# A chunk's transposed outputs in the bytes of its own sums

## The chip, the cores and the metric

The kernel runs on one core of a Trainium2 chip. The metric is the time of one execution in device microseconds, the median of several runs. Besides, one execution was taken by the hardware profiler; its trace is what the rows below are from.

## What is computed

Two independent blocks share the launch, and their outputs stand side by side. Block A is sliding-window attention over 2048 tokens, 32 heads of 32 columns, a window of 256 keys; block B is a Fourier mixing by matrix products.

```python
q, k, v = split(x @ wqkv)                       # x: 2048 x 1024
scores = (q @ k.T) * Dh ** -0.5                 # mask: 0 <= query - key < 256
a = (softmax(scores) @ v) @ wo
y = re(DFT_seq) @ (xb @ DFT_hid_re.T) - im(DFT_seq) @ (xb @ DFT_hid_im.T)
out = concatenate([a, y], axis=-1)
```

## The kernel before

The big products (q, k and v, then block B, then `wo`) are float16 products of split operands: each float32 operand is a high and a low half, and three passes of 128x512 matmuls make one product. The attention is a generator, `attention()`, which `tick` advances between these matmuls, a step every few matmuls by a rate per unit. So the attention's instructions are woven into the stream of each engine in an order that the code fixes; TensorE works through its list in that order.

The attention goes over *blocks* (g, hp, sc, i): eight groups g of four heads, two head pairs hp, four chunks sc of 512 queries, four blocks i of 128 queries. Four blocks that share (g, hp, sc) make a *chunk*; there are 64 chunks and 256 blocks. For each block b:

- `s_step`: TensorE makes the scores of both heads (`s`, and `far` for the oldest key block; two halves of one bank alternate as `far`), VectorE masks them with `far` (`copy_predicated`, L259) and takes the row maximum, ScalarE takes exponentials and the high half, VectorE the low half (`hl`, L275), and a DMA issued from SP transposes both into `t` (L277).
- `z_step`: GpSimd masks two triangles (`z`, L289, and `t`, L291).
- `v_step`, six blocks later (`LAG`) and for two blocks at once: TensorE multiplies with v into `pv`, and VectorE reduces the halves into the chunk's sums `o` (L323). A chunk has two such reduces; the first one allocates `o`.
- `o_step`, right after a chunk's second reduce: VectorE takes the reciprocals of the row sums (L332), GpSimd multiplies (L334), ScalarE takes the high half (L337) and GpSimd the low half (L338) into `ohl`, a DMA issued from SP transposes `ohl` into `ot` (L340).
- The store of `ot` to DRAM (`ots`, L360) is issued from SP about three blocks later, at the next block with i = 3. The last chunks' stores follow at once.

`o`, `ohl` and `ot` are tiles of the pool `att` under one tag, `"o"`, with three buffers of 1056 bytes per partition. Which of the three a tile gets is decided while the program is built. In the program before, `ohl` is always in the same buffer, and `o` and `ot` share the other two: for most chunks all `o` lie in one and all `ot` in the other, and at some chunks they change places, `ot` lying where the chunk's own `o` lay. A tile that takes a buffer over waits until the last instructions that used the buffer are done: the store for `ot`, and GpSimd's subtraction (L338) for `o`.

SP issues all loads, transpositions and most stores, in the order of the code; a wait in it holds up what stands behind. After the attention and block B, the pool `late` takes the memory of `att`, and the product with `wo` ends the kernel.

Of the kernel before, what the change touches and what calls it, by code (L numbers as in the profile page):

```python
# [9 lines left out]
F32 = mybir.dt.float32  # L10
F32R = mybir.dt.float32r
F16 = mybir.dt.float16
# [7 lines left out]
P = 128  # L20
# [3 lines left out]
DH = 32  # L24
# [6 lines left out]
QB = CH // P  # L31
# [22 lines left out]
def fused_kernel(ctx: ExitStack, tc: tile.TileContext, xa, wqk, wv, wo, xb, wd, cs, out):  # L54
    nc = tc.nc
# [57 lines left out]
    def mm(*args, **kwargs):  # L113
        with tc.issue_after(fixed[0].ins) if fixed else nullcontext():
            fixed[:] = [nc.tensor.matmul(*args, **kwargs)]  # L115
        return fixed[0]
# [94 lines left out]
    def attention():  # L211
        att = cell["att"]
# [3 lines left out]
        st, cur, q2s, k2s, vts, store_o = {}, {}, {}, {}, {}, []  # L216
# [78 lines left out]
        def v_step(b):  # L295

            g, hp, sc, i = blocks[b]
            pvb = ps_v.tile([P, CH], F32, tag="pv", name=f"pv_{b}")
            pvt = pvb[:, :4 * VW].rearrange("p (r h w) -> p r h w", r=2, h=2)
            if (g, hp, sc) not in cur:  # L300
                cur[g, hp, sc] = att.tile([P, QB, 2, DH + 1], F32, tag="o", bufs=3, name=f"o_{g}_{hp}_{sc}")
            for r in (1, 0):
                qb = sc * QB + i + r
                nb = min(qb + 1, 3)
                nt = min(nb, 2)
                d = st[b + r]

                def weights(part, j, kb):
                    if nb == 3 and kb == 0:
                        return d["z"][:, part * 2 + j]  # L310
                    return d["t"][:, (part * 2 + j) * nt + kb - (nb - nt)]

                seq = [(0, kb) for kb in range(nb)] + [(1, kb) for kb in range(nb)]
                for j in range(2):
                    at = j * VW
                    for m, (part, kb) in enumerate(seq):
                        w = VW if part == 0 else DH + 1
                        k = qb + 1 - nb + kb
                        mm(pvt[:, r, j, :w], weights(part, j, kb),
                           vts[g, hp, k // QB][:, k % QB, at:at + w],  # L320
                                         start=(m == 0), stop=(m == len(seq) - 1),
                                         skip_group_check=True)
            nc.vector.tensor_reduce(cur[g, hp, sc][:, i:i + 2], pvt.rearrange("p r h (k w) -> p r h w k", k=2),  # L323
                                    axis=AX.X, op=ALU.add)
            del st[b], st[b + 1]

        def o_step(g, hp, sc):

            o = cur.pop((g, hp, sc))
            rs = att.tile([P, 2 * QB], F32, tag="rs", name=f"rs_{g}_{hp}_{sc}")  # L330
            on = o.rearrange("p i h w -> p (i h) w")
            nc.vector.reciprocal(rs, on[:, :, DH])  # L332
            on = on[:, :, :DH]
            nc.gpsimd.tensor_tensor(on, on, rs.unsqueeze(2).to_broadcast([P, 2 * QB, DH]), op=ALU.mult)  # L334
            o = o[:, :, :, :DH]
            ohl = att.tile([P, QB, 2, DH, 2], F16, tag="o", bufs=3, name=f"ohl_{g}_{hp}_{sc}")
            nc.scalar.activation(ohl[:, :, :, :, 0], o, AF.Copy)  # L337
            nc.gpsimd.tensor_tensor(ohl[:, :, :, :, 1], o, ohl[:, :, :, :, 0], op=ALU.subtract)  # L338
            ot = att.tile([P, QB, P], F16, tag="o", bufs=3, name=f"ot_{g}_{hp}_{sc}")
            nc.sync.dma_start_transpose(ot, ohl.rearrange("p i h d a -> p (i h d a)"))  # L340
            store_o.append((ots[sc, g, hp].rearrange("c a t -> (c a) t"), ot.rearrange("p i q -> p (i q)")))

        for b in range(nblk + LAG):
            for j in range(2):
                yield (blocks[b][0], blocks[b][2]) if b < nblk else None
                if b < nblk and j == 0:
                    s_step(b, 0)
                    s_step(b, 1)
                if j == 1 and b % 2 == 0 and b >= LAG:
                    v_step(b - LAG)  # L350
                    g, hp, sc, i = blocks[b - LAG + 1]
                    if i == QB - 1:
                        o_step(g, hp, sc)
                if j == 1 and b % 2 == ZAT and 3 <= b < nblk + 4:
                    for m in (b - 3 - (ZAT == 0), b - 2 - (ZAT == 0)):
                        if 0 <= m < nblk:
                            z_step(m)
                if j == 1 and store_o and (b >= nblk or blocks[b][3] == 3):
                    with tc.issue_after(line[0].ins):
                        nc.sync.dma_start(*store_o.pop(0))  # L360
                if j == 1 and b < nblk and blocks[b][3] == 1 and b + 3 < nblk:
                    g, hp, sc, _ = blocks[b + 3]
                    if (g, sc) in ready:
                        do_load(g, hp, sc)
                if j == 1 and b < nblk and blocks[b][3] == 3 and b + 1 < nblk:
                    g, hp, sc, _ = blocks[b + 1]
                    if (g, sc) in ready:
                        do_load_v(g, hp, sc)
# [526 lines left out]
    with tc.tile_pool(name="pa", bufs=3) as pa:  # L895
# [43 lines left out]
        for n, (kd, g, c) in enumerate(order):  # L939
# [12 lines left out]
            if kd == "v":  # L952
# [6 lines left out]
                f = vf[:, g, t // 4:t // 4 + 1]  # L959
# [137 lines left out]
    with tc.tile_pool(name="pb", bufs=1) as pb:  # L1097
# [45 lines left out]
        for n, (kind, p, c, i) in enumerate(units):  # L1143
# [35 lines left out]
            f = fu.pop(n)  # L1179
# [75 lines left out]
```

## Time and profile before

| | us |
|---|---|
| median of 3 runs | 1704.11 |
| lowest and highest of them | 1701.39, 1705.67 |
| the profiled execution | 1701.5 |
| its span in the trace | 1699.8 |
| TensorE busy in the span | 1688.6 |
| VectorE busy | 1299.0 |
| ScalarE busy | 1168.5 |
| GpSimd busy | 575.2 |

The span runs from the first to the last instruction of the program; the profiled execution's time is 1.7 us more. TensorE's matmuls overlap in its pipeline, so that their own durations (379 ns as a mean for 128x512) are longer than the distance from one to the next; how fast TensorE goes is read from starts. The mean granted clock of the profiled execution is 1.00 of full speed.

### The profile page before, as it was taken

What the parts mean: (1) busy time and instruction counts of PE and PEld (TensorE: products, weight loads), DVE (VectorE), ACT (ScalarE), POOL (GpSimd) and SP (SyncE); (2) the same over time, 40 slices, a digit from 0 to 9 for tenths busy, and PEclk for the clock granted to TensorE, in tenths of its full rate; (3) what the DMA queues carried; (4) which work ended last, traced back from release to release, by engine and by line L of the source; (5) the groups of instructions that cost most, each with busy time, mean ns of one, the idle gap of its engine ahead of it and who ended that gap; (6) DMA issues with size and microseconds to landing.
All of it is one profiled execution on the core that took longest, in us unless ns stands there. A gap on an engine that the chain in (4) does not pass through costs nothing.

```text
span 1699.8 us, 30887 instructions
## 1 busy us (share of the span) xinstructions
PE 1688.6 (99%) x11007; PEld 847.7 (50%) x11007; DVE 1299.0 (76%) x2223; ACT 1168.5 (69%) x2035; POOL 575.2 (34%) x874
## 2 busy tenths in 40 slices
PE   9999999999999999999999999999999999999999
PEld 4444544555555555555554555545545545444444
DVE  7657787888987789897688896688876698687442
ACT  4476666676876787887787886688877688563322
POOL 0001222344434441444423565434555425411000
PEclk9999999999999999999999999999999999999999
DMA  6677999999999985987997999986989976866431
GB/s 244 240 267 245 252 289 269 282 264 306 256 240 209 211 220 127 206 194 184 232 251 236 199 186 176 227 197 127 190 161 204 226 183 137 177 180 121 115 99 75
DMA packets 469899, 348.63 MB, mean 205 GB/s; under 512 B 376944, under 2 KB 409968, under 8 KB 468848
## 3 DMA queue, kind: packets, MB, share of 16 engines
q1 hardware_dynamic: 462064, 321.48, 75.7%
q0 software_dynamic: 7680, 25.17, 9.5%
q8 instruction: 86, 1.41, 0.4%
q14 instruction: 69, 0.57, 0.1%
HBM read 166.99 MB, written 106.17 MB: 161 GB/s over the span
## 4 chain that ended last, share of the span: by engine, by line
PE 90%; DVE 3%; DMA 3%; ACT 2%; issue 1%; SPq 0%; POOL 0%; DVEq 0%; ACTq 0%; POOLq 0%
PE p_a L115 25%; PE pv L115 13%; PE p_b L115 12%; PE pq L115 10%; PE pk L115 10%; PE p_c L115 6%; PE po_a L115 5%; PE s L115 3%; PE po_b L115 2%; PE far L115 1%; PE po_c L115 1%; DMA ots<-ot 1%; DMA raw_wo<-in_wo_dram 1%; DVE reg L850 0%; DMA t<-hl 0%
## 5 line engine op out<-in xcount | busy, mean ns | idle before, releaser
L271 ACT ACTIVATE s<-s,bias,escs 128x256 f32<-128x256 f32 (+1 forms) x512 | 270.0, 528 | 11.7
L289 POOL TENSOR_SCALAR_AFFINE_SELECT z<-t 128x512 f16<-128x512 f16 x224 | 183.8, 828 | 162.2 <-PE pv L115 140.3
L264 ACT ACTIVATE bias<-mx,pshift,escs 128x2 f32<-128x2 f32 x256 | 98.4, 384 | 172.0 <-DVE mx L261 171.3
L275 DVE TENSOR_TENSOR hl<-s,hl 128x512 f16<-128x512 f32 (+1 forms) x256 | 170.2, 665 | 51.6 <-ACT hl L274 50.8
L115 PEld LDWEIGHTS <-reg 128*128 128x128 f16 x1344 | 128.9, 98 | 141.5
L291 POOL TENSOR_SCALAR_AFFINE_SELECT t<-t 128x512 f16<-128x512 f16 x224 | 187.8, 847 | 11.3
L115 PE MATMUL p_a<-reg,un_c 128*128 128x512 f16 x768 | 181.4, 379 | 0.6 <-DVE reg L850 0.3
L115 PE MATMUL pk<-reg,wu_k 128*128 128x512 f16 x768 | 174.2, 379 | 0.0
L268 POOL TENSOR_SCALAR mark<-bias 128x1 f32<-128x1 f32 x128 | 52.5, 410 | 358.3 <-ACT bias L264 333.6
L261 DVE TENSOR_REDUCE mx<-s 128x2 f32<-128x512 f32 (+1 forms) x256 | 170.9, 668 | 3.5
L115 PE MATMUL pv<-reg,reg 128*128 128x512 f16 x768 | 172.5, 379 | 0.0
L115 PEld LDWEIGHTS <-un_c 128*128 128x128 f16 x1152 | 109.9, 97 | 121.5 <-issue 2.2
L115 PEld LDWEIGHTS <-un_b 128*128 128x128 f16 x1152 | 109.6, 97 | 117.7 <-issue 0.9
L115 PEld LDWEIGHTS <-un_a 128*128 128x128 f16 x1152 | 109.4, 97 | 116.5
L115 PE MATMUL pq<-reg,wu_q 128*128 128x512 f16 x696 | 156.3, 379 | 0.0
L274 ACT ACTIVATE hl<-s 128x512 f16<-128x512 f32 (+1 forms) x256 | 148.8, 581 | 6.9 <-DMA t<-hl 1.4
L115 PE MATMUL p_a<-reg,un_b 128*128 128x512 f16 x576 | 136.4, 379 | 0.3 <-DVE y L1045 0.2
L115 PE MATMUL p_c<-reg,un_a 128*128 128x512 f16 x576 | 136.5, 379 | 0.0
L115 PE MATMUL p_b<-reg,un_b 128*128 128x512 f16 x576 | 136.3, 379 | 0.1
L115 PE MATMUL p_a<-reg,un_a 128*128 128x512 f16 x576 | 136.1, 379 | 0.0
L259 DVE COPY_PREDICATED s<-upper,far 128x256 f32<-128x256 uint32 x224 | 94.3, 421 | 46.3 <-PE s L115 45.3
L115 PEld LDWEIGHTS <-qk 96*128 96x128 f16 x1056 | 87.7, 97 | 66.4 <-issue 4.9
(216 smaller groups left out, 3139.7 us busy)
## 6 DMA issues: line engine op xcount, KB each, us to landing
raw_u<-in_cs_dram SPq DMA_DIRECT2D x64, 512.0 KB, 5.0
qk<-qk SPq DMA_DIRECT2D x64, 384.0 KB, 4.7
out_dram<-y POOLq DMA_DIRECT2D x72, 256.0 KB, 6.3
raw_wd<-in_wd_dram SPq DMA_DIRECT2D x24, 512.0 KB, 5.6
vs<-yv SPq DMA_DIRECT2D x32, 264.0 KB, 4.5
vt<-vs SPq DMA_DIRECT2D x64, 132.0 KB, 4.7
qk<-yq SPq DMA_DIRECT2D x32, 256.0 KB, 4.5
raw_wo<-in_wo_dram SPq DMA_DIRECT2D x16, 512.0 KB, 8.4
```

What stands on the lines that cost most here:

```text
L115: fixed[:] = [nc.tensor.matmul(*args, **kwargs)]
L259: nc.vector.copy_predicated(s[:, :, P:], upper2, d["far"] if nb == 3 else never2)
L261: nc.vector.tensor_reduce(mx, sv, axis=AX.X, op=ALU.max, negate=True)
L264: nc.scalar.activation(bias, mx, AF.Identity, bias=pshift, scale=es)
L268: marks[:] = [nc.gpsimd.tensor_scalar(mark, bias[:, 0:1], 1.0, None, op0=ALU.mult)]
L271: nc.scalar.activation(sv[:, h], sv[:, h], AF.Exp, bias=bias[:, h:h + 1], scale=es)
L274: nc.scalar.activation(hi, sv, AF.Copy)
L275: behind[:] = [nc.vector.tensor_tensor(lo, sv, hi, op=ALU.subtract)]
L289: nc.gpsimd.affine_select(out=z, in_=pk, compare_op=ALU.is_gt, fill=0.0, base=0, pattern=[[0, 4], [-1, P]], channel_multiplier=1)
L291: nc.gpsimd.affine_select(out=pk, in_=pk, compare_op=ALU.is_ge, fill=0.0, base=0, pattern=[[0, 4], [1, P]], channel_multiplier=-1)
```

## The change

The tile `o` becomes a ring of two, and `ot` is no tile of its own any more: it is a float16 view of the first 1024 bytes of the chunk's own `o`. `ohl` gets a tag of its own with one buffer. The arithmetic is the same.

```diff
-                cur[g, hp, sc] = att.tile([P, QB, 2, DH + 1], F32, tag="o", bufs=3, name=f"o_{g}_{hp}_{sc}")
+                cur[g, hp, sc] = att.tile([P, QB * 2 * (DH + 1)], F32, tag="o", bufs=2, name=f"o_{g}_{hp}_{sc}")
...
-            nc.vector.tensor_reduce(cur[g, hp, sc][:, i:i + 2], pvt.rearrange("p r h (k w) -> p r h w k", k=2),
+            o = cur[g, hp, sc].rearrange("p (i h w) -> p i h w", i=QB, h=2)
+            nc.vector.tensor_reduce(o[:, i:i + 2], pvt.rearrange("p r h (k w) -> p r h w k", k=2),
                                     axis=AX.X, op=ALU.add)
...
-            o = cur.pop((g, hp, sc))
+            held_o = cur.pop((g, hp, sc))
+            o = held_o.rearrange("p (i h w) -> p i h w", i=QB, h=2)
...
-            ohl = att.tile([P, QB, 2, DH, 2], F16, tag="o", bufs=3, name=f"ohl_{g}_{hp}_{sc}")
+            ohl = att.tile([P, QB, 2, DH, 2], F16, tag="ohl", bufs=1, name=f"ohl_{g}_{hp}_{sc}")
...
-            ot = att.tile([P, QB, P], F16, tag="o", bufs=3, name=f"ot_{g}_{hp}_{sc}")
+            ot = held_o.bitcast(F16)[:, :QB * P].rearrange("p (i q) -> p i q", i=QB)
             nc.sync.dma_start_transpose(ot, ohl.rearrange("p i h d a -> p (i h d a)"))
```

On every engine the instructions stand in the same order before and after; what changes is what they wait for. The first place is SP's queue at the end of the attention, before the change; the names end in hp, sc and a number of the buffer, the brackets name the semaphores (DMAHW0 to DMAHW7 count landed DMAs, eight in turn), and `ot_1_1` is the output of chunk (7,1,1).

```order
L277 DMA_TRANSPOSE t_18468<-hl_18465 128x8x128 [waits DMAHW4_49,DVE_49,PE_49]
L360 DMA ots<-ot_1_1_18300 128x512 [waits DMAHW7_49]
L340 DMA_TRANSPOSE ot_1_2_18543<-ohl_1_2_18540 128x4x128 [waits DMAHW6_49,DMAHW5_49,Pool_49]
L360 DMA ots<-ot_1_2_18543 128x512 [waits DMAHW6_49]
L768 DMA raw_u_0_18769<-in_cs_dram 128x1024 [waits DMAHW0_49,DVE_49]
```

The same place in the changed program, where the transposed output is `o`:

```order
L277 DMA_TRANSPOSE t_18406<-hl_18403 128x8x128 [waits DMAHW4_49,DVE_49,PE_49]
L362 DMA ots<-o_1_1_18081 128x512 [waits DMAHW7_49,DMAHW5_49]
L342 DMA_TRANSPOSE o_1_2_18342<-ohl_1_2_18478 128x4x128 [waits DMAHW6_49,DVE_49,Pool_49]
L362 DMA ots<-o_1_2_18342 128x512 [waits DMAHW6_49]
L770 DMA raw_u_0_18705<-in_cs_dram 128x1024 [waits DMAHW0_49,DVE_49]
```

The transposition of chunk (7,1,2) waited for DMAHW5, the store issued just ahead of it, and does not any more. The second place is VectorE's list at the first reduce of the last chunk, (7,1,3), before the change:

```order
L787 TENSOR_SCALAR fu_18591<-fa,sc_u_18585 128x1
L122 SCALAR_TENSOR_TENSOR un_a<-raw_u_0_18309,sc_u_18585,un_a 128x1024 [waits DMAHW2_49,Activation_49]
L323 TENSOR_REDUCE o_1_3_18610<-pv_18609 128x132 [waits PE_49,Pool_49]
L807 TENSOR_TENSOR raw_u_0_18309<-raw_u_0_18309,raw_u_1_18127 128x512 [waits DMAHW3_49,DVE_49]
L807 TENSOR_TENSOR raw_u_1_18127<-raw_u_1_18127 128x512 [waits DVE_49]
L122 SCALAR_TENSOR_TENSOR reg_83<-raw_u_1_18127,sc_u_18585,reg_83 128x512 [waits Activation_49]
```

And in the changed program:

```order
L789 TENSOR_SCALAR fu_18528<-fa,sc_u_18522 128x1
L122 SCALAR_TENSOR_TENSOR un_a<-raw_u_0_18247,sc_u_18522,un_a 128x1024 [waits DMAHW2_49,Activation_49]
L324 TENSOR_REDUCE o_1_3_18547<-pv_18546 128x132 [waits DMAHW5_49,DMAHW7_49,PE_49,Pool_49]
L809 TENSOR_TENSOR raw_u_0_18247<-raw_u_0_18247,raw_u_1_18066 128x512 [waits DMAHW3_49,DVE_49]
L809 TENSOR_TENSOR raw_u_1_18066<-raw_u_1_18066 128x512 [waits DVE_49]
L122 SCALAR_TENSOR_TENSOR reg_83<-raw_u_1_18066,sc_u_18522,reg_83 128x512 [waits Activation_49]
```

The reduce now also waits for the two DMAs that last used its tile: the transposition into it (DMAHW7) and the store out of it (DMAHW5), both of chunk (7,1,1).

## Rows read from the trace of the kernel before

**Rows 1.** The page: busy time, share of the span, instructions.
```profile
PE 1688.6 (99%) x11007; PEld 847.7 (50%) x11007; DVE 1299.0 (76%) x2223; ACT 1168.5 (69%) x2035; POOL 575.2 (34%) x874
```
**Rows 2.** Chain that ended last, 1265 to 1300 us: start, us, what.
```profile
1273.10 0.11 PE s L115
1273.21 3.45 PE p_a L115 x16
```
**Rows 3.** Waits of TensorE, longest first: us in total, times, longest.
```profile
PE far L115 <- DVE s L259: 4.3, 2, 3.2
PE wps L735 <- DVE reg L727: 1.2, 1, 1.2
PE p_a L115 <- DVE y L1045: 0.5, 2, 0.3
```
**Rows 4.** Chain that ended last, 1220 to 1245 us.
```profile
1227.53 9.63 DMA ots<-ot
...
1237.18 0.05 DVEq L323
1237.23 0.05 issue
```
**Rows 5.** Timeline of VectorE and TensorE, 1231 to 1241 us: start, duration, [idle before].
```profile
1237.38 0.43 DVE L323 TENSOR_REDUCE o<-pv 128x132 f32<-128x264 f32 x1 [5.70 <-DMA ots<-ot]
...
1239.53 0.42 DVE L259 COPY_PREDICATED s<-upper,far 128x256 f32<-128x256 uint32 x1
...
1240.01 0.22 PE L115 MATMUL far<-qk,qk 96*128 96x128 f16 x1 [3.21 <-DVE s L259]
```
**Rows 6.** Waits of SP's queue, two of them.
```profile
SPq L277 <- DVE hl L275: 131.4, 64, 14.0
...
SPq L340 <- DMA ots<-ot: 42.0, 26, 5.7
```
**Rows 7.** Waits of VectorE, one of them.
```profile
DVE o L323 <- POOL ohl L338: 0.8, 1, 0.8
```
**Rows 8.** Tile o: its reduces, ns min/median/max, first and last start in us.
```profile
L323 DVE TENSOR_REDUCE o<-pv x128: 417/424/434, 170.6 to 1470.0; 128x132 f32<-128x264 f32 x128
```
**Rows 9.** Line L360: the stores, and us from issue to landing.
```profile
L360 SPq DMA_DIRECT2D ots<-ot x64: 319/570/2020, 202.8 to 1476.9; - x64
...
DMA to landing us min/median/max: 1.9/3.6/9.6
```
**Rows 10.** One store (tile ot, 526 us), its landing, and the reduce (timeline).
```profile
L360 SPq DMA_DIRECT2D ots<-ot x1: 570/570/570, 526.2 to 526.2; - x1
...
DMA to landing us min/median/max: 3.3/3.3/3.3
...
531.23 0.42 DVE L323 TENSOR_REDUCE o<-pv 128x132 f32<-128x264 f32 x1
```
**Rows 11.** Timeline of SP, VectorE and TensorE, 1454 to 1480 us.
```profile
1458.97 0.57 SPq L360 DMA_DIRECT2D ots<-ot  x1
...
1462.50 0.43 DVE L323 TENSOR_REDUCE o<-pv 128x132 f32<-128x264 f32 x1
...
1465.33 1.19 SPq L340 DMA_TRANSPOSE ot<-ohl  x1
1465.46 0.80 DVE L122 SCALAR_TENSOR_TENSOR reg<-raw_u,sc_u,reg 128x512 f16<-128x512 f32 x1 [1.21 <-ACT reg L128]
...
1472.36 2.75 PE L115 MATMUL p_b<-reg 128*128 128x512 f16 x12
```
**Rows 12.** Landing of t's transposition at 721 us, then of ot's at 722.
```profile
DMA to landing us min/median/max: 2.3/2.3/2.3
...
DMA to landing us min/median/max: 2.4/2.4/2.4
```
**Rows 13.** Windows, 600 to 1450 us: busy by engine, PEclk, DMA share, GB/s.
```profile
600.00:1450.00 850.00, 845.64 (x5983) 435.79 (x5982) 693.93 (x1230) 663.53 (x1210) 374.11 (x520) 1.00 0.90 193
```
**Rows 14.** Tile t: us from issue to landing of its 256 transpositions.
```profile
DMA to landing us min/median/max: 2.3/4.7/11.4
```

## The prediction

> **What bounds the kernel now.** I read the busy times first: TensorE is busy for 1688.6 of 1699.8 us [rows 1]. A busy share alone can hide a slow engine, so the next view is the chain that ended last: sixteen 512-column matmuls take 3.45 us, 0.216 us each, in the middle of the attention, right behind a score matmul and with nothing between [rows 2]. TensorE runs its list back to back; what can be won is only what it waits. Its waits come next [rows 3]: 4.3 us in two waits for VectorE's masking of the scores (L259), 1.2 us at the start, and then rows of 0.5 us and less. So the reader is to see a kernel that no buffer change can speed by more than about 4.3 us, and that can lose whatever a new wait passes on to TensorE.
>
> Where the first of the two waits comes from is the key to this change. At 1227.53 the store of chunk (6,0,2)'s transposed output is issued and takes 9.63 us to land [rows 4]. The first reduce of chunk (6,1,0) writes the buffer that this store reads, and VectorE stood 5.70 us until 1237.38; the masking queued behind it ran at 1239.53, and TensorE waited 3.21 us for it [rows 5]. So a late store costs TensorE its lateness less 2.5 us (5.70 - 3.21).
>
> **The change, part by part.**
>
> *Removed: the transposition's wait for the store of the chunk before.* Before, sums and transposed outputs mostly held one tile each, so the transposition of chunk n (L340) had to wait for the store of chunk n-1. The queue stood 42.0 us for it in 26 waits, at most 5.7 us [rows 6]. These go. Queued behind them on SP are the next blocks' transpositions, loads of raw_u, q/k and v. The same queue stands 131.4 us just for VectorE's halves of the weights [rows 6], so it catches up by itself, and no TensorE wait names a load or transposition of the attention [rows 3]. I take 0 us as the gain. The other end: all 42.0 us cannot come back, since the PE waits cap it at 4.3 us.
>
> *Removed: the reduce's wait for GpSimd's subtraction of the chunk before* (its tile is free only when L338 has read it). VectorE stood 0.8 us for it, once [rows 7]. The 2.5 us of slack above covers it: 0 us.
>
> *Added: the first reduce of chunk n waits for the store of chunk n-2.* Two tiles, each held from a chunk's first reduce until its store has landed. In the built program with its semaphores, 62 of the 64 first reduces wait on a DMA now, 10 before; for 52 of them it is a store that they did not wait for. Chunks follow each other every 20.5 us (128 reduces, two a chunk, from 170.6 to 1470.0 [rows 8]), a store is issued some three blocks before the reduce, and the 64 stores land in 3.6 us as a median, 9.6 at most [rows 9]. I laid each of the 52 stores beside its reduce, at the times of before. In 51 the store had landed at least 1.7 us earlier; the closest is the reduce of chunk (2,0,1) at 531.23, whose store was issued at 526.2 and landed 3.3 later [rows 10]. One is late, the last chunk: store at 1458.97, landed when the transposition behind it starts, 1465.33, while the reduce started at 1462.50 [rows 11]: 2.8 us of VectorE. Queued behind it is the subtraction of raw_u and the split of reg that ended at 1466.26; TensorE first uses reg at 1472.36 [rows 11], so 2.8 us is covered by 6.1 us. Without that cover it would cost 2.8 us. The transposition of (7,1,2) in turn no longer waits and starts some 4.8 us earlier, so the end of the attention is not later. The wait of 5.70 us at chunk (6,1,0) is on the same store before and after: nothing gained there, 0 us.
>
> *Added: waits as such.* 35 more on VectorE, 47 on GpSimd, 39 on SP stand as instructions of their own. In the trace a satisfied wait shows as 0.05 us of VectorE's queue and 0.05 us to the next [rows 4], so 3.5 us of VectorE over 64 chunks, 0.05 us in each, 4.7 on GpSimd, 3.9 on SP. VectorE is busy 1299.0 of 1699.8 [rows 1]: hidden. GpSimd's new wait at L334 is for the store that VectorE's reduce has already seen: 0.
>
> *Unchanged:* the halves (ohl) had one buffer in practice before as well, and the order on every engine is the same row for row.
>
> *Moved in memory.* A third buffer of 1056 bytes becomes one of 1024, so the other tiles of the pool move by 32 bytes, hl and t among them; both began at multiples of 256 bytes in the built program, and no longer do. The nearest row: the ot transposition reads and writes at addresses off such multiples before too, and lands in 2.4 us for the same 128x512 elements that a first block's t takes 2.3 us for, side by side at 721 and 722 us [rows 12]. I take that 0.1 us, on a transposition nothing in TensorE waits for: 0 us. The Trainium skill (DMA: Bandwidth & Descriptors, section "How a descriptor splits into AXI transactions") speaks against the change here: a descriptor that does not start at a 256-byte address costs extra beats. By that rule each 256-byte row would take nine beats for eight, an eighth more; the two rows above show at most a twenty-third, and the measurement decides.
>
> **Sum** against the profiled execution (span 1699.8, time 1701.5 us): -0 (queue) -0 (GpSimd) +0 (last chunk) +0 (waits) +0 (address) = 1701.5. That execution lies 2.6 us under the median of the three timed runs, 1704.11, for which the forecast is the same: **1704 us**. What a measurement can tell here from no change is 0.3%, 5.1 us.
>
> **Rivals.**
>
> *Late stores (slower).* Ten reduces waited on a DMA before and one was 5.70 us late; if the 52 new ones behave like those ten, five more are late, 5 x 3.2 = 16 us, 1720 us. For it: the landings spread from 1.9 to 9.6 us [rows 9], the stretch from 600 to 1450 us has its DMA engines busy 0.90 of the time [rows 13], and another execution deals the landings out differently. Against it: side by side only one is late. It decides from a landing more than 2.5 us after the reduce is ready, and needs two such in a run: 1704.1 + 2 x 3.2 = 1710.5 us. Chance 0.09.
>
> *The freed queue pays (faster).* If earlier transpositions and loads take away both waits for L259 and the 2.6 us by which the median exceeds the profiled execution, 1704.1 - 4.3 - 2.6 = 1697.2 us. For it: 26 queue waits gone. Against it: the longer of the two waits hangs on a store that the change keeps, so at most 1.1 us of rows 3 is open to it. Chance 0.07.
>
> *Addresses (slower).* With the DMA engines at 0.90 [rows 13] a rise of 4% (0.1 of 2.3 us) gives 0.94 and nothing; from 11% on (1/0.90) they would be full, and the first per cent beyond costs 1% of the 1300 us between the first and the last reduce, 13 us: 1717 us. The page named above (the Trainium skill, DMA: Bandwidth & Descriptors) has the rule by which this would happen, and its eighth is about that first per cent; the trace does not agree as far as rows 12 reach. Chance 0.04.
>
> **How the numbers follow.** The forecast has 0.80, and its own range is 1700 to 1708, the spread of the three runs with little added. Range 1699 to 1711 us: it takes in the two late stores and most of a gain; outside are more late stores, full DMA engines and the whole of the freed queue, some 0.12. Faster 0.07, same 0.80, slower 0.09 + 0.04 = 0.13.
>
> **What would show it.** Right: the queue's wait of L340 for ots gone; VectorE's reduce waiting for ots a few times, a few us in all, at the last chunk among them; TensorE's waits for L259 near 4 us again. Wrong: waits of TensorE for L259 above 10 us with stores named behind them (late stores), a median of t's landing well over the 4.7 us of before [rows 14] (addresses), or no wait for L259 at all (the queue paid).

## The result, and the profile after

The changed kernel takes 1712.43 us (median of 8 runs, 1706.83 to 1718.6) where the kernel before, on the same chip, takes 1704.2 (8 runs, 1701.24 to 1707.13): ratio 1.005 [1.0028, 1.0071]. It is slower by half a per cent; the forecast of 1704 and the upper end of the range, 1711, are both below it. The profiled execution took 1715.21 us with a span of 1713.5.

The page of the changed kernel, span and busy times; the second row answers to [rows 1].
```profile
span 1713.5 us, 31008 instructions
...
PE 1695.1 (99%) x11007; PEld 849.6 (50%) x11007; DVE 1300.1 (76%) x2223; ACT 1170.8 (68%) x2035; POOL 574.7 (34%) x874
```
TensorE is busy 6.5 us longer with the same 11007 instructions, and the span is 13.7 us longer. The medians lie only 8.2 us apart; what follows is read from these two executions, of which the changed one is slower than its median and the other faster. There are two things to look for: new waits, and the same matmuls at a lower clock. Waits of TensorE, changed kernel (us in total, times, longest), which answer to [rows 3]:
```profile
PE far L115 <- DVE s L259: 6.3, 2, 5.1
PE pv L115 <- DVE o L324: 3.0, 1, 3.0
PE pv L115 <- DVE sc_u L122: 2.6, 1, 2.6
PE wps L737 <- DVE reg L729: 1.2, 1, 1.2
```
With four smaller rows the waits come to 14.1 us; those of before came to 6.8 in all. Two of the rows are new. The clock is in the windows; their columns are the stretch, its length, busy us of TensorE, its weight loads, VectorE, ScalarE and GpSimd, the granted clock, the DMA share and GB/s. Changed kernel: the stretches behind its three waits, 2 us within the second of them, and the three stretches in which the transfers ran that these waits hang on:
```profile
962.00:967.00 5.00, 4.84 (x39) 2.40 (x39) 4.41 (x9) 4.90 (x10) 4.11 (x6) 0.66 0.79 170
1246.00:1253.00 7.00, 6.14 (x27) 2.79 (x27) 6.21 (x12) 4.93 (x10) 2.94 (x4) 0.51 0.66 112
1481.00:1486.00 5.00, 4.82 (x36) 2.31 (x36) 4.83 (x11) 1.15 (x1) 0.52 (x1) 0.66 0.12 33
1248.00:1250.00 2.00, 2.00 (x6) 0.61 (x5) 1.97 (x4) 2.00 (x4) 1.96 (x3) 0.50 0.56 70
936.00:956.00 20.00, 20.00 (x145) 10.30 (x144) 15.63 (x30) 14.75 (x29) 9.05 (x14) 1.00 1.21 172
1230.00:1242.00 12.00, 11.72 (x71) 5.73 (x70) 4.78 (x11) 7.55 (x15) 3.30 (x5) 1.00 1.15 205
1467.00:1484.00 17.00, 14.03 (x103) 6.84 (x102) 5.21 (x11) 7.41 (x13) 5.53 (x8) 0.93 1.01 160
```
Behind the three waits the granted clock is 0.66, 0.51 and 0.66 as a mean, and 0.50 within: TensorE runs for some us at the lower of its two levels, 1.2 GHz instead of 2.4. By an estimate from these rows that costs 5 x 0.34 + 7 x 0.49 + 5 x 0.34 = 6.8 us, near the 6.5 us of longer busy time. The waits grew by 7.3 us (14.1 less 6.8); with the clock's 6.8 that makes 14.1, against 13.7 us of longer span. What this execution lost lies in three places.

The last three rows show what is special there. The DMA share is above 1 in all three stretches, which means that packets overlap on the engines. The same stretches of the kernel before, counted from the same issues and equally long:
```profile
935.50:955.50 20.00, 20.00 (x145) 10.27 (x144) 16.70 (x33) 16.35 (x31) 11.49 (x17) 1.00 1.22 205
1225.20:1237.20 12.00, 11.60 (x70) 5.69 (x69) 4.66 (x10) 7.99 (x15) 5.11 (x8) 1.00 1.09 224
1458.00:1475.00 17.00, 17.00 (x123) 8.45 (x122) 10.13 (x18) 9.96 (x15) 7.03 (x10) 1.00 0.79 179
```
In two of the three the share had been above 1 before as well (1.22 and 1.09), although its mean over 850 us is 0.90 [rows 13]. At the same or a higher share the engines now move less: 172 GB/s for 205, 205 for 224, and at the tail 160 with a share of 1.01 for 179 with 0.79. The transfers there take more of the engines' time for what they move.

How that reaches TensorE stands in the timeline of the changed kernel (start, duration, [idle before, and its releaser]):
```profile
944.34 5.81 SPq L277 DMA_TRANSPOSE t<-hl  x1
955.86 0.38 ACT L274 ACTIVATE hl<-s 128x256 f16<-128x256 f32 x1 [2.58 <-DMA t<-hl]
955.89 0.63 POOL L289 TENSOR_SCALAR_AFFINE_SELECT z<-t 128x512 f16<-128x512 f16 x1 [6.16 <-PE pt_u L176]
962.16 0.19 PE L115 MATMUL pv<-vt,z 128*128 128x66 f16 x1 [2.56 <-DVE sc_u L122]
...
1232.41 1.75 POOL L1138 DMA_DIRECT2D out_dram<-y  x2
1232.51 0.60 SPq L362 DMA_DIRECT2D ots<-o  x1
1233.21 4.90 SPq L277 DMA_TRANSPOSE t<-hl  x1
1244.23 0.43 DVE L324 TENSOR_REDUCE o<-pv 128x132 f32<-128x264 f32 x1 [7.63 <-DMA ots<-o]
1246.38 0.42 DVE L259 COPY_PREDICATED s<-upper,far 128x256 f32<-128x256 uint32 x1
1246.86 0.27 PE L115 MATMUL far<-qk,qk 96*128 96x128 f16 x1 [5.13 <-DVE s L259]
...
1467.24 1.67 POOL L1138 DMA_DIRECT2D out_dram<-y  x2
1468.15 0.55 SPq L362 DMA_DIRECT2D ots<-o  x1
1480.69 0.43 DVE L324 TENSOR_REDUCE o<-pv 128x132 f32<-128x264 f32 x1 [8.96 <-DMA ots<-o]
1481.18 0.19 PE L115 MATMUL pv<-vt,z 128*128 128x66 f16 x1 [2.98 <-DVE o L324]
```
The chain that ended last has both stores in it:
```profile
1232.51 11.60 DMA ots<-o
...
1468.15 12.36 DMA ots<-o
```
At each place GpSimd's stores that add into the output (out_dram<-y, L1138) and transpositions are in flight together; at the second and the third the store of a chunk is with them. The store of 1232.51 is chunk (6,0,2)'s, the late one of [rows 4]; it took 9.63 us before and takes 11.60 now. VectorE waited 7.63 us for it where it had waited 5.70 [rows 5], and TensorE 5.13 where it had waited 3.21. At 1468.15 it is the store for which the last chunk's reduce waits, 12.36 us in place of the 6.36 from its issue at 1458.97 to the transposition behind it at 1465.33 [rows 11]. At 944.34 it is no store but a transposition: it landed 11.4 us later, at 955.7, just when GpSimd went on; its mask, then the normalising of a chunk, ScalarE and VectorE followed late, and the matmuls of pv at 962.16 with them. (GpSimd's row names pt_u, which ended in the same 0.1 us; ScalarE's row beside it names the transposition.) The same transposition before landed after 6.3 us, and of the 5.1 us between them 3.5 went by while SP was still issuing it:
```profile
943.81 2.30 SPq L277 DMA_TRANSPOSE t<-hl  x1
```

### The profile page after: what moved, and what is told of

The parts are those of the page before. It is cut to its first block, busy times and chain, and to the rows that moved or that the text cites. A ratio compares the mean times of both kernels' runs of the same rounds, so it can differ in the third digit from the quotient of the medians.

```text
span 1713.5 us, 31008 instructions
## 1 busy us (share of the span) xinstructions
PE 1695.1 (99%) x11007; PEld 849.6 (50%) x11007; DVE 1300.1 (76%) x2223; ACT 1170.8 (68%) x2035; POOL 574.7 (34%) x874
## 4 chain that ended last, share of the span: by engine, by line
PE 88%; DMA 4%; DVE 3%; ACT 3%; issue 1%; SPq 0%; POOL 0%; DVEq 0%; POOLq 0%; ACTq 0%
PE p_a L115 24%; PE pv L115 13%; PE p_b L115 12%; PE pq L115 10%; PE pk L115 10%; PE p_c L115 6%; PE po_a L115 5%; PE s L115 3%; PE po_b L115 2%; DMA ots<-o 2%; PE far L115 1%; PE po_c L115 1%; DMA raw_u<-in_cs_dram 1%; DVE reg L852 1%; DMA raw_wo<-in_wo_dram 1%
## 5 line engine op out<-in xcount | busy, mean ns | idle before, releaser
L259 DVE COPY_PREDICATED s<-upper,far 128x256 f32<-128x256 uint32 x224 | 94.3, 421 | 51.3 <-PE s L115 49.6
```

What stands on the lines that cost most here:

```text
L259: nc.vector.copy_predicated(s[:, :, P:], upper2, d["far"] if nb == 3 else never2)
```

## Experiments

The theory after these rows: **the addresses**. The tiles that moved by 32 bytes make transfers dearer. The rival: **the ring**. The new waits of the reduces for stores are what costs. Each part can be had without the other. Ratios are to the kernel before on the same chip, as recorded over all runs (a quotient of the medians differs from them by up to 0.0007): 1702.83 us (30 runs) beside ring2_old_addresses, before_new_addresses, three_tiles and ring2_store_early; 1703.29 (29 runs) beside ring2_old_early, three_tiles_new_addresses, hl_off and t_off; 1702.02 (21 runs) beside hl_off_128, both kernels with plain stores and three_tiles_aligned.

**ring2_old_addresses**: the change, with 32 bytes of padding. In the built program qk, vt, hl, t and o lie where they lay before the change; z, rs and ohl do not.
```diff
-            ohl = att.tile([P, QB, 2, DH, 2], F16, tag="ohl", bufs=1, name=f"ohl_{g}_{hp}_{sc}")
+            ohl = att.tile([P, QB * 2 * DH * 2 + 16], F16, tag="ohl", bufs=1, name=f"ohl_{g}_{hp}_{sc}")[:, :QB * 2 * DH * 2].rearrange(
+                "p (i h d a) -> p i h d a", i=QB, h=2, d=DH)
```


> The changed kernel with ohl's tile 32 bytes longer, so that every other tile of the pool lies where it lay before the change; all waits of the change stay. Theory A, late stores (the first reduce waits for the store of two chunks before, and a late store is passed on to TensorE): as slow as the change, some 1712 us, 1.004 to 1.006 of the kernel before; VectorE's reduce waits for ots by 10 us or more. Theory B, addresses (rows of hl and t off multiples of 256 bytes make the DMA engines slower): the loss goes, 1704 us, within 0.1% of before; t's shortest full landing is 2.7 us again and not 3.0. If both have a part, between them.

Measured: 1704.25 us (12 runs), 1.0014 [0.9999, 1.0028]. The loss is gone but for what cannot be told from no change. Its waits of TensorE and of VectorE, one row each, and the row of VectorE in the changed kernel:
```profile
PE far L115 <- DVE s L259: 4.6, 2, 3.4
```
```profile
DVE o L324 <- DMA ots<-o: 8.7, 2, 5.8
```
```profile
DVE o L324 <- DMA ots<-o: 16.6, 2, 9.0
```
The reduces wait for two stores here as well, but 8.7 us instead of 16.6, and TensorE's row is near that of before, 4.3 [rows 3]. So where the landings are short, the waits of the ring cost little more than the one such wait of the kernel before.

**before_new_addresses**: the kernel before, with padding that puts hl, t, qk and o where the change puts them within 256 bytes.
```diff
-            z = att.tile([P, 4, P], F16, tag="z", bufs=3, name=f"z_{b}")
+            z = att.tile([P, 4 * P + 16], F16, tag="z", bufs=3, name=f"z_{b}")[:, :4 * P].rearrange("p (a q) -> p a q", a=4)
-            rs = att.tile([P, 2 * QB], F32, tag="rs", name=f"rs_{g}_{hp}_{sc}")
+            rs = att.tile([P, 2 * QB + 16], F32, tag="rs", name=f"rs_{g}_{hp}_{sc}")[:, :2 * QB]
```


> The kernel before with 224 bytes more in its pool (longer z and rs tiles), so that hl, t, qk and o begin at the same remainder by 256 bytes as in the change; all waits are those of before. Theory A: as before, 1704 us, 0.999 to 1.001. Theory B: as slow as the change, 1712 us, 1.004 to 1.006, t's shortest full landing 3.0 us. Both: between.

Measured: 1708.75 us (7 runs), 1.0038 [1.0022, 1.0054]. Padding alone makes the kernel before slower, at the same places: TensorE waits 7.7 us for L259 (4.3 before) and 1.7 for sc_u, and its waits come to 12.5 us. The addresses are the larger part; 1.0038 and 1.0014 together are 1.0052, against 1.005.

**hl_off, t_off, hl_off_128**: which of the tiles? The kernel before with padding, so that of hl and t hl alone (what the transpositions read) lies 32 bytes off a multiple of 256, t alone (what they write), or hl 128 bytes off (padding of 32 floats for 56).
```diff
+            if b == 0:
+                att.tile([P, 56], F32, tag="pad", bufs=1, name="pad")
```
(hl_off; behind hl's tile. t_off has 8 floats there, and z and rs as in before_new_addresses.)

> The kernel before with hl alone (what the transposition reads) 32 bytes past a multiple of 256, t at a multiple. By the page's rule, which is told for reads: t's shortest full landing 3.0 us and 1.003 to 1.004. If the writes cost: 2.7 us and 1.000.

> The kernel before with t alone (what the transposition writes) 32 bytes past a multiple of 256, hl at a multiple. If the reads cost: shortest full landing 2.7 us and 1.000. If the writes cost: 3.0 us and 1.003 to 1.004. If each has a part, both this and the run with hl moved lie at 2.8 to 2.9 us.

> The kernel before with hl 128 bytes past a multiple of 256. If a second transaction for each row is what costs: t's shortest full landing 3.0 us as at 32 bytes, and 1.003 to 1.004. If the beats cost (12 for 8 by the page, 9 for 8 at 32 bytes): above 3.5 us and slower than at 32 bytes. If only remainders under 64 cost: 2.7 us and 1.000.

Measured: hl_off 1709.49 us (6 runs), 1.0042 [1.0026, 1.0057]; t_off 1703.18 (12 runs), 1.0003 [0.9991, 1.0014]; hl_off_128 1709.19 (5 runs), 1.004 [1.0026, 1.0055]. It is the address that the transpositions read from, and 128 bytes off cost what 32 do. In the built programs the tiles ahead of hl move with it, among them qk and vt, which loads write; they lay off multiples of 256 before too, and their shortest landings stay (qk 1.7 us in all three, vt 2.2 to 2.3). A single transposition shows it where no other transfer is issued beside it, tile t at 696 us, of the kernel before and of hl_off:
```profile
L277 SPq DMA_TRANSPOSE t<-hl x1: 1232/1232/1232, 696.4 to 696.4; - x1
...
DMA to landing us min/median/max: 2.7/2.7/2.7
```
```profile
L279 SPq DMA_TRANSPOSE t<-hl x1: 1232/1232/1232, 696.3 to 696.3; - x1
...
DMA to landing us min/median/max: 3.0/3.0/3.0
```
It takes 3.0 us also in the changed kernel and in hl_off_128, and 2.7 in t_off: about a ninth more, from the source alone. The Trainium skill (DMA: Bandwidth & Descriptors, section "How a descriptor splits into AXI transactions") has a transaction begin at a 256-byte address, so that a row that does not begin there takes one transaction more and the beats fetched in vain. The runs agree that such a start costs; by an estimate in that page's beats, 128 bytes off (twelve for eight) would cost far more than 32 (nine for eight), and that the runs do not show.

**plain_stores, plain_stores_hl_off**: does it take GpSimd's adding stores beside it? They are made plain ones, in the kernel before and in hl_off. This leaves out the sums over the halves of block B.
```diff
-                nc.gpsimd.dma_start(dst, src, accum_op=ALU.add)
+                nc.gpsimd.dma_start(dst, src)
```


> The kernel before with GpSimd's accumulating stores of the Fourier block replaced by plain ones (the sums over the halves of that block are left out). It is the base for the next run: TensorE's work is the same, some reading of DRAM goes; 1699 to 1704 us.

> The same plain stores, and hl 32 bytes past a multiple of 256. If the cost of the address needs the accumulating stores beside the transpositions (all places where t lands late are of that kind): within 0.1% of the run with plain stores and hl at a multiple, no landing of t above 11 us. If it does not: 0.3 to 0.4% above it.

Measured: 1696.91 us (6 runs), 0.9967 [0.9955, 0.998], faster than the 1699 to 1704 expected, and with hl off 1697.08 (5 runs), 0.997 [0.9958, 0.9982]. Without the adding stores the address costs 0.0003, nothing that can be told; the single transposition of above still takes 3.0 us with hl off and 2.7 without. One detail of the second expectation missed: a landing of t of 12.6 us remains. Windows of plain_stores_hl_off, the long stretch of [rows 13] and the three places:
```profile
600.00:1450.00 850.00, 848.92 (x6023) 437.79 (x6021) 692.43 (x1236) 668.83 (x1216) 353.65 (x527) 1.00 0.85 193
933.00:953.00 20.00, 20.00 (x147) 10.43 (x146) 16.68 (x33) 16.44 (x33) 10.32 (x17) 1.00 1.00 213
1223.00:1239.00 16.00, 16.00 (x99) 8.10 (x98) 12.77 (x24) 12.47 (x25) 7.52 (x13) 1.00 1.11 220
1456.00:1473.00 17.00, 17.00 (x124) 8.45 (x122) 11.16 (x19) 7.46 (x11) 4.65 (x7) 1.00 0.55 149
```
The DMA share is lower (0.85 for 0.90, and 1.00 for 1.22 and 0.55 for 0.79 at the first and the last place); the middle one is at 1.11 (over 16 us) for 1.09 (over 12). TensorE is busy without a gap in all three, and its longest wait for L259 is 0.8 us.

**three_tiles, three_tiles_new_addresses, three_tiles_aligned**: what do a reduce's waits for stores cost? Here sums, halves and outputs have one tile each. No reduce waits for a store, and each transposition of the outputs waits for the store before it. The first has the addresses of before, the second (a padding tile of 32 bytes, rs as it was) those of the change, and the third has ohl and ot at multiples of 256 as well.
```diff
-                cur[g, hp, sc] = att.tile([P, QB, 2, DH + 1], F32, tag="o", bufs=3, name=f"o_{g}_{hp}_{sc}")
+                cur[g, hp, sc] = att.tile([P, QB, 2, DH + 1], F32, tag="o", bufs=1, name=f"o_{g}_{hp}_{sc}")
-            rs = att.tile([P, 2 * QB], F32, tag="rs", name=f"rs_{g}_{hp}_{sc}")
+            rs = att.tile([P, 2 * QB + 8], F32, tag="rs", name=f"rs_{g}_{hp}_{sc}")[:, :2 * QB]
-            ohl = att.tile([P, QB, 2, DH, 2], F16, tag="o", bufs=3, name=f"ohl_{g}_{hp}_{sc}")
+            ohl = att.tile([P, QB, 2, DH, 2], F16, tag="ohl", bufs=1, name=f"ohl_{g}_{hp}_{sc}")
-            ot = att.tile([P, QB, P], F16, tag="o", bufs=3, name=f"ot_{g}_{hp}_{sc}")
+            ot = att.tile([P, QB, P], F16, tag="ot", bufs=1, name=f"ot_{g}_{hp}_{sc}")
```


> o, ohl and ot each in one buffer of their own for all chunks, addresses of hl and t as before: no reduce waits for a store at all, and every transposition waits for the store of the chunk before. Theory A: no reduce waits for ots, TensorE's long wait near 1240 us goes, so 1700 to 1704 us, 0.998 to 1.000. Theory B says nothing but as before, 1.000. Theory C (the SP wait that the change removes kept transpositions apart from stores, and its loss makes stores late) has no landing of a store above 10 us here.

> Three tiles with one buffer each (no reduce waits for a store) and hl, t, qk and o at the remainders of the change. Theory B (late landings of the transpositions themselves reach TensorE through z and pv, without any store): 1.002 to 1.004, t's longest landings above 12 us, waits of TensorE for pv. If the addresses cost only by making the stores late that a reduce waits for: 0.998 to 0.999, as with three tiles at the old addresses.

> Three tiles with one buffer each, and not only hl and t but also ohl and ot at multiples of 256 bytes. If reads off a multiple cost, ot's shortest landing falls from 2.4 us to some 2.3 or less, and the time is at or a little under that of three tiles: 0.997 to 0.999.

Measured: 1699.93 us (11 runs), 0.9982 [0.9974, 0.9991]; 1705.64 (12 runs), 1.0021 [1.0009, 1.0034]; 1699.83 (12 runs), 0.9985 [0.9975, 0.9995]. Waits of TensorE and of SP's queue in three_tiles:
```profile
PE far L115 <- DVE s L259: 1.0, 1, 1.0
```
```profile
SPq L340 <- DMA ots<-ot: 56.2, 33, 5.1
```
The queue waits 56.2 us for stores, more than the 42.0 of [rows 6], and the kernel is faster than the kernel before and than the change: the wait is harmless on SP and costs on VectorE. Aligning ohl and ot too gives nothing more in time; the shortest landing of the outputs' transposition goes from 2.4 to 2.3 us, as expected. In three_tiles_aligned:
```profile
DMA to landing us min/median/max: 2.3/4.0/9.2
```
At the change's addresses the loss is back although no reduce waits for a store; TensorE then waits for sc_u (4.7 us in two waits).

**ring2_store_early, ring2_old_early**: the change with a chunk's store issued at an earlier block, so that no reduce finds it under way; the second with the old addresses too.
```diff
-                if j == 1 and store_o and (b >= nblk or blocks[b][3] == 3):
+                if j == 1 and store_o and (b >= nblk or blocks[b][3] == 1):
```


> The changed kernel, new addresses and all, with each chunk's store issued two blocks earlier on SP (at a block with i = 1 and not i = 3), some 10 us more between a store and the reduce that waits for it. Theory A: the reduces no longer wait, the loss goes, 1703 to 1706 us, 0.999 to 1.001. Theory B: as slow as the change, 1712 us. Theory C: stores still late beside transpositions, with landings above 10 us, but less of it reaches VectorE.

> The changed kernel with both repairs: old addresses (ohl's tile 32 bytes longer) and each store issued two blocks earlier. If addresses and late stores are the two causes and nothing else is lost: 1699 to 1703 us, 0.998 to 1.000, no reduce waits for ots, TensorE waits for L259 1 us or so, as with three tiles. If the early transposition beside the stores costs by itself (theory C): 1.002 or more.

Measured: 1709.2 us (12 runs), 1.0031 [1.0014, 1.0048]; with the old addresses 1701.63 (12 runs), 0.9993 [0.998, 1.0007]. In neither does a reduce wait for a store. Waits of TensorE in ring2_store_early, from an execution of 1715.9 us, longer than its median:
```profile
PE pv L115 <- POOL z L289: 4.6, 1, 4.6
PE pv L115 <- DVE sc_u L122: 4.0, 1, 4.0
PE p_a L115 <- ACT y L1045: 2.0, 1, 2.0
```
Most of the loss is left and has changed its way: the transposition of t at 1463.9 landed after 16.5 us, and TensorE waits for the mask behind it. So earlier stores do not cure the addresses, and with the old addresses they cost nothing.

**Together.** The new addresses of hl and t against the old, the waits being equal, by dividing the ratios:
```
kernel                     new / old addresses
before                     1.0038
the change                 1.0050 / 1.0014 = 1.0036
the change, early store    1.0031 / 0.9993 = 1.0038
three tiles                1.0021 / 0.9982 = 1.0039
plain stores (hl alone)    0.9970 / 0.9967 = 1.0003
```
Whichever wait passes it on, the address costs some 0.4%, about 6 us, as long as the adding stores are there. That the four agree so closely is luck: each ratio has an interval of 0.001 to 0.002 to either side, and from the medians they come to 1.0031 to 1.0047. The rival is left with 1.0014 [0.9999, 1.0028], which is not clearly apart from no change. That is so because the kernel before waits for a late store too. Against the same kernel without such waits they cost about 0.2%: 1.0014 / 0.9993 and 1.0050 / 1.0031 for the ring at the old and the new addresses, 1 / 0.9982 for the kernel before. The first two are hardly more than their intervals, the third is twice its own.

## Why the prediction was wrong, point by point

- **Removed waits: right.** SP's wait of L342 (L340 before) for ots is gone, the queue's other waits grew (in all it waits 1051 us before and 1047 now, although the 42.0 are gone), and nothing came back of the 42.0 us. GpSimd's wait by L338 cost nothing.
- **Added waits of the reduces: right in kind.** One chunk more is late, the last, and (6,1,0) as before. At (6,1,0) the rule that TensorE pays a store's lateness less 2.5 us held to the digit: 7.63 - 5.13 = 2.50.
- **The last chunk: right for the old addresses, by a wrong path.** Forecast were 2.8 us of waiting for the reduce and 0 for TensorE. In ring2_old_addresses that came: the store lands after 6.3 us although the transposition now starts 1.5 us behind it, the reduce waits 2.82 us, and no wait of TensorE names it.
```profile
1460.96 0.53 SPq L363 DMA_DIRECT2D ots<-o  x1
...
1462.50 2.37 SPq L343 DMA_TRANSPOSE o<-ohl  x1
...
1467.41 0.43 DVE L324 TENSOR_REDUCE o<-pv 128x132 f32<-128x264 f32 x1 [2.82 <-DMA ots<-o]
```
At the change's addresses the wait became 8.96, and TensorE waited 2.98 us for the reduce, by another way than the split of reg and its use: the pool of pv has one bank, and its next matmuls must wait until the reduce has read it. This way covers 8.96 - 2.98 = 5.98 us; that the forecast's cover was 6.1 is luck.
- **"Moved in memory": the step that failed.** Its term, +0 (address), measured about 6 us (1.0036 to 1.0039 new against old). It took 0.1 us, from 2.3 and 2.4 us of a single pair of transpositions of half the size [rows 12], and let that decide. The full transposition goes from 2.7 to 3.0 us, three times that. Worse was the cover, "a transposition nothing in TensorE waits for: 0 us". It was read from a trace in which no wait of TensorE hung on such a landing, while the store of (6,0,2), which TensorE did wait for, is in flight with such transpositions.
- **The rival "addresses" asked the wrong average.** It held that engines at 0.90 [rows 13] leave room until 11%. That is a mean over 850 us; 20 us of it stood at 1.22 already, and it is in such stretches that transpositions and stores landed late. The rival "late stores" had its point right (two late ones, 1710.5 us) and comes near the measured 1712.43 by luck: it reckoned with the old landings, and with these the same two waits gave 1704.25 (ring2_old_addresses). What came is both, the one by the other. The signs named for either did not show: t's median stayed, and only its end grew, with TensorE's waits for L259 at 6.3 us, not above 10.
- **The price of a wait was half of it.** The prediction counted a wait's own us; in the profiled execution the stretches at the lower clock behind the waits cost nearly as much again, an estimated 6.8 us to 7.3.

Landing of t's 256 transpositions in the changed kernel, which answers to [rows 14]: the median is 0.1 us lower and the longest 1.5 us longer.
```profile
DMA to landing us min/median/max: 2.4/4.6/12.9
```
The longest landing alone does not tell the loss either. In three_tiles, at the old addresses and without any loss, it is longer:
```profile
DMA to landing us min/median/max: 2.3/5.0/14.8
```
What counts is whether something that TensorE needs stands behind a late landing.

What stays open: why transpositions that take a ninth longer by themselves cost the kernel 0.4% beside GpSimd's adding stores and nothing that can be told beside plain ones. DMA shares above 1 are what the windows show at these places, but that alone does not settle it: with plain stores and hl off the middle place stands at 1.11 and the address costs nothing. Whether the adding stores lengthen the landings, or only leave TensorE less time to spare, was not measured apart.

## What to carry to other kernels

A tile that changes its size moves its neighbours in the pool: look at the addresses of everything that a DMA transposition reads, keep them at multiples of 256 bytes, and test a buffer change once more with padding that puts the rest back. Ask whether transfers may become dearer in the stretches where the DMA share is highest, not over its mean, and read the landings behind which something waits that TensorE needs, neither the median nor the longest. Let a wait for a store stand on the queue that has time (three_tiles, 0.9982) rather than on an engine that TensorE waits for.

## What the runs showed of the hardware that was not expected

- A transposition of 128x1024 float16 elements that reads from 32 or from 128 bytes past a multiple of 256 takes 3.0 us for 2.7 where no other transfer is issued beside it; one that writes 32 bytes past takes 2.7.
- The same address costs the kernel 0.4% beside GpSimd's adding stores and 0.03% (not to be told from 0) beside plain ones.
- A wait of TensorE of a few us was mostly followed by a stretch at 1.2 GHz, but not always: behind 2.56, 5.13 and 2.98 us in the changed kernel the clock was 0.66, 0.51 and 0.66, behind 3.4 us in ring2_old_addresses 0.68 from 1240 to 1244, and behind 3.21 us in the kernel before 1.00 from 1240 to 1247.
